# Order of work ahead of the first row gather in a sketch-attention and router kernel

## The chip, the core and the metric

The kernel runs on one core of a Trainium2 chip. The metric is the device time of one launch, in microseconds (us); lower is better. Each engine (TensorE, VectorE, ScalarE, GpSimd, SyncE; PE, DVE, ACT, POOL and SP in the profile) works through its own instruction queue in order. An instruction whose inputs are not ready holds up everything behind it in the same queue.

## What is computed

`q`, `k` and `v` have 4 batches, 4 heads, 1088 tokens and 32 numbers per head. `S1` and `S2` are 8x32 sketches. Attention has no softmax: each key and query becomes 64 features, the products of its 8 numbers under S1 with its 8 under S2. The result has 4352 rows of 128 numbers, and each row goes to one of 8 experts.

```
q_p, k_p = phi(q), phi(k)                    # phi(x)[i*8+j] = (S1 x)[i] * (S2 x)[j]
kv = einsum('bhsf,bhsd->bhfd', k_p, v);  z = sum(k_p, axis=2)
x = (q_p @ kv) / (q_p @ z + 1e-6)            # 4352 rows of 128
logits = (x/|x|) @ (emb/|emb|).T / tau       # 8 experts
e = argmax(logits);  gate = softmax(logits)[e]
out[row] = gate * (relu(x[row] @ w1[e]) @ w2[e])     # w1: 128x1024, w2: 1024x128
```

## The kernel before, in words

**Halves.** Two batches are worked on at a time, so the attention comes in halves m=0 (batches 0, 1) and m=1 (batches 2, 3). In each half the tokens are 17 tiles of 128, taken in groups that begin at tile c0 = 0, 4, 8, 12 (four tiles each) and 16 (one tile). The text writes "group 4" for the group that begins at tile 4.

**A group of queries** goes through these steps in `queries` (L485): `tr` (L494) turns the queries on PE and copies them on ACT; `ab` (L500) multiplies by the sketches; `b` (L505) copies the second factors on ACT (groups 0 and 8 of half 1 copy both factors, L381); `prod` (L512) multiplies the factors, on DVE, or on POOL for groups 0 and 8 of half 1 (L386); `tr_qp` (L538) turns the features on PE (L542) and `qpT` (L545) copies them on ACT (L547); `nd` (L549) multiplies by the sums of the keys on PE (L555); `x` (L562) divides on DVE (L565 to L572). In half 0 the four large groups go another way: `pairs` (L515) makes both factors of all 64 features directly on PE (L522), `seconds` (L527) copies the second factors on ACT (L531), and `prods` (L533) multiplies on DVE (L534).

**Routing.** `router` (L628) picks the expert of each row, counts rows per expert, and `place` (L648) gives each row its place in its expert. A first table (`table(0, ...)`, L726) is made from half 0 alone. It lists the rows of 10 full blocks of 128 rows each with one expert; a second table with 28 blocks comes later, from all rows. The first table's chain is `place` (L654 to L658), `count` (L786, L779), `take` and `split` (L661, L665), `rest` (L789, with `blocks`, L699), `mark` (L674), `find` (L736, the line L744), `digit` twice (L748), `sums` on PE (L754) and `tokens` (L765, three DVE instructions L769 to L771). `tokens` writes two lists of indices: `dst_i`, where an empty lane has the number 8192, and `src_i`, the same cut off at the last row.

**Experts.** `fetch` (L882) gathers the 128 rows of a block from DRAM by an indirect DMA of POOL (L885), `turn` (L889) turns them on PE (L891) and copies them (L893), `up` (L931) is the first layer (L939 on PE, the ReLU L947 on ACT), `down` (L969) the second (L975, L984) and the scatter of the result (L987, which leaves out indices above the last row). The gate comes from `norm` (L949: ACT L952, then a power on POOL, L953), `inverse` (L955, DVE L956 and L957), `shares` (L959, ACT L963) and `share` (L965, DVE).

**What sets the order.** `put_at(tick)(after, rank, f)` (L997) files a piece of work under a tick and a rank. `emit` (L1085) issues the ticks in order and, in a tick, the pieces by rank. Each engine's queue has its instructions in that order. Around the change the pieces are:

- tick 8: turn group 4 of half 1 (53.5), the last keys, `total`, turn group 8 (55.3), `tr_qp` of group 0 (55.5), `tr_kv`, `ab` of group 4 (55.8), `place` (56), `count` (56.5), `take`, `split`, `qpT` of group 0 (58), `rest`, `b` of group 4 (58.7), `mark`, `find`, the two digits, `prod` of group 4 (62.5), turn groups 12 and 16, `nd` of group 0 (84), `ab`, `b` and `prod` of group 8 (84.6 to 84.8), `sums` (85), `tokens` (86), the gathers 0 to 3 (87), `x` of group 0 (90);
- tick 9: `tr_qp` and `qpT` of group 4 (20), `ab` and `b` of groups 12 and 16 (21), `tr_qp` and `qpT` of group 8 (21.5), `nd` of group 4 (30), `turn(0)` (30.21), `nd` of group 8 (30.3), `norm(0)` (30.7), `prod` of groups 12 and 16 (30.8), `x` of group 4 (71) and of group 8 (71.5);
- tick 10: gather 4 (29), `up(0)` (30), `turn(1)` (45), `inverse(0)` (59), `shares(0)` (60), `best` and `pick` for half 1 (72), `norm` of blocks 1 to 3 (74.6);
- tick 11: `tr_qp` and `qpT` of groups 12 and 16 (20), gather 5, `up(1)` (30), `turn(2)` (45), `nd` of groups 12 and 16 (70), `place`, `down(0)` (74).

**PSUM.** The large tiles, `ps_big` (L90), have two buffers, which are taken in turn: each new tile takes the buffer of the tile before the last. `pairs`, `tr_qp` of a large group, `nd`, the table's bank and `up` all take one.

Of the kernel before, what the change touches and what calls it, by code (L numbers as in the profile page):

```python
# [11 lines left out]
F32 = mybir.dt.float32  # L12
BF16 = mybir.dt.bfloat16
I32 = mybir.dt.int32
# [32 lines left out]
NOWHERE = 8192  # L47
# [16 lines left out]
def kernel(  # L64
# [32 lines left out]
    zeros = consts.tile([P, P], F32, name="zeros")  # L97
# [3 lines left out]
    def keep_warm(n):  # L101
        for _ in range(n):
            nc.tensor.matmul(ps_warm[:, :P], zeros, zeros, start=True, stop=True)  # L103
# [15 lines left out]
    nc.scalar.dma_start(tau_sb[:], bass.AP(tensor=tau.tensor, offset=tau.offset, ap=[[0, E], [1, 1]]))  # L119

# [107 lines left out]
    rows = tc.dram_tile([N, ROW], F32, name="rows")  # L228
# [27 lines left out]

    def more_constants():
        nc.vector.memset(ones, 1.0 / P)
        nc.vector.memset(ones_e, 1.0)

        nc.vector.memset(less, -(P - 1) / (2.0 * P))
        nc.vector.memset(more, (P - 1) / (2.0 * P))

        nc.vector.memset(near, -1.0 / (2.0 * P))
        nc.vector.memset(c_early, 0.0)
        nc.vector.memset(w_late, float(KEYS * E))
        for t in (place_k, place_r):
            nc.vector.memset(t, -1.0)

    def iotas():  # L270
# [22 lines left out]
        nc.vector.tensor_copy(digits, tok_i[:, 1:])  # L293
# [191 lines left out]
    def queries(m, c0, c1, put, put_nd):  # L485
# [41 lines left out]
        def seconds(j):  # L527
            if j == 0:
                s["b"] = tile_of(n, [P, 2, w], "qpT")
                s["qpT"] = held[:, c0 // 4].rearrange("p (a n) -> p a n", a=2)  # L530
            nc.scalar.copy(s["b"][:, j].rearrange("p (j n) -> p j n", j=2), s["big"][j][:, :, 2 * P:])  # L531

        def prods(j):  # L533
            nc.vector.tensor_mul(s["qpT"].rearrange("p a (j n) -> p j a n", j=4)[:, 2 * j:2 * j + 2],  # L534
                                 s["big"][j][:, :, :2 * P].rearrange("p j (a n) -> p j a n", a=2),
                                 s["b"][:, j].rearrange("p (j a n) -> p j a n", j=2, a=2))
# [53 lines left out]
        else:  # L590
# [102 lines left out]
    src_i = [consts.tile([P, n], I32, name=f"src_i{i}") for i, n in enumerate(SIZES)]  # L693
# [32 lines left out]
    def table(which, m1, key):  # L726
# [6 lines left out]
        def lie(t):  # L733
            return t if which == 0 else t.rearrange("p n w -> p w n")

        def find():  # L736
            if which == 0:
                s["hit"] = consts.tile([P, n, w], BF16, name="hit0")
                s["col"] = consts.tile([P, 2, n, w], BF16, name="col0")
            else:  # L740

                s["hit"] = work.tile([P, w, n], BF16, tag="xg", bufs=3, name="hit1").rearrange("p w n -> p n w")
                s["col"] = work.tile([P, w, 2, n], BF16, tag="xg", bufs=3, name="col1").rearrange("p w d n -> p d n w")
# [21 lines left out]
        def tokens(k0, k1):  # L765
            ps = s["ps"].rearrange("p (d n) -> p d n", d=2)
            rest = column(f"rest{which}_{k0}", w=k1 - k0)
            to = dst_i[which][:, k0:k1]
            nc.vector.tensor_scalar(rest, ps[:, 1, k0:k1], -1.0, float(NOWHERE), op0=ALU.mult, op1=ALU.add)  # L769
            nc.vector.tensor_sub(to, rest, ps[:, 0, k0:k1])  # L770
            nc.vector.tensor_scalar_min(src_i[which][:, k0:k1], to, N - 1)  # L771
# [110 lines left out]
    def fetch(i):  # L882
# [3 lines left out]
            out=xs[i][:], out_offset=None, in_=rows[:2 * S if t == 0 else N],  # L886
            in_offset=bass.IndirectOffsetOnAxis(ap=src_i[t][:, j:j + 1], axis=0))

    def turn(i):  # L889
# [3 lines left out]
        (nc.scalar.copy if i == 0 or 4 <= i <= 8 else nc.vector.tensor_copy)(xT[i], ps[:, :P])  # L893
# [135 lines left out]
    put(0, 87, lambda: [fetch(i) for i in range(AHEAD)])  # L1029
# [110 lines left out]
```

## Time and profile before

| what | value |
|---|---|
| median of 9 runs | 205.7 us (204.2 to 207.36) |
| the profiled execution's own time | 204.62 us |
| its span, first to last instruction | 202.8 us |
| outside the span | 1.8 us |
| granted TensorE clock | 0.995 |
| busy: PE, DVE, ACT, POOL | 193.8, 91.6, 101.9, 105.5 us |
| bytes moved | 39.42 MB, mean 194 GB/s |

All times in the text that are points on the clock are microseconds from the span's start. The profile gives, for each engine, when instructions began and how long they took (timeline), what an engine waited for (waits), and the chain of waits that ended last, followed back from the last instruction. "x32" after a line is a count of instructions; a matmul on f32 shows as two.

### The profile page before, as it was taken

How to read it: one execution, taken by the hardware profiler on the slowest of the kernel's cores; microseconds unless marked ns; L12 is line 12 of the kernel's file. 1: busy time of each engine (PE TensorE's matmuls, PEld its weight loads, DVE VectorE, ACT ScalarE, POOL GpSimd, SP SyncE). 2: the span in 40 equal slices, each digit the busy share in tenths (PEclk: the TensorE clock that was granted, in tenths of full speed). 3: DMA queues.
4: the chain of work that ended last, by engine and by line, in shares of the span. 5: the costliest groups of instructions: out<-in, count | busy, mean ns of one | idle time of the engine just before them, and what ended most of it. 6: DMA issues, size and time to landing. Idle time of an engine off the chain costs nothing.

```text
span 202.8 us, 6985 instructions
## 1 busy us (share of the span) xinstructions
PE 193.8 (96%) x2592; PEld 183.2 (90%) x2592; DVE 91.6 (45%) x402; ACT 101.9 (50%) x290; POOL 105.5 (52%) x136
## 2 busy tenths in 40 slices
PE   7989999998899999999999999999999999999991
PEld 7658778987799999999999999999999999999991
DVE  5577858978884759942221221222212212112200
ACT  2656442254446546634555554654555546777440
POOL 4010100332745567757786767767767677564043
PEclk9999999999999999999999999999999999999997
DMA  4999899981669478664566466565665796485000
GB/s 124 328 266 313 200 286 278 269 302 39 146 236 290 176 242 263 173 180 106 189 179 205 151 188 192 157 203 172 154 224 150 187 306 238 104 302 196 3 26 25
DMA packets 28160, 39.42 MB, mean 194 GB/s; under 512 B 5737, under 2 KB 21364, under 8 KB 28128
## 3 DMA queue, kind: packets, MB, share of 16 engines
q1 hardware_dynamic: 25776, 34.23, 56.6%
q0 software_dynamic: 2304, 4.74, 7.7%
q8 instruction: 22, 0.36, 0.8%
q14 instruction: 10, 0.08, 0.1%
q10 hardware_dynamic: 48, 0.01, 0.0%
HBM read 34.37 MB, written 4.73 MB: 193 GB/s over the span
## 4 chain that ended last, share of the span: by engine, by line
PE 83%; ACT 4%; DVE 4%; DMA 3%; POOL 3%; issue 1%; POOLq 0%; ACTq 0%; DVEq 0%
PE ps_big L939 27%; PE ps_acc L975 14%; PE ps_ab L975 14%; PE ps_big L944 4%; PE ps_acc L439 4%; PE ps_big L555 3%; DMA xs<-rows,src_i 3%; PE ps_t L353 3%; PE ps_t L891 2%; PE ps_big L522 2%; PE ps_acc L978 2%; PE ps_ab L978 2%; PE ps_ab L370 2%; PE ps_acc L103 1%; ACT qpT L531 1%
## 5 line engine op out<-in xcount | busy, mean ns | idle before, releaser
L939 PE MATMUL ps_big<-xTb,wb 128*128 128x128 f32 x512 | 62.9, 276 | 0.0
L939 PEld LDWEIGHTS ps_big<-xTb,wb 128*128 128x128 f32 x512 | 59.7, 192 | 0.6 <-DVE gate L967 0.2
L987 POOL DMA_INDIRECT out_dram<-y,dst_i x36 | 37.4, 1040 | 41.0 <-ACT y L984 19.9
L947 ACT ACTIVATE hT<-ps_big 128x1024 f32<-128x1024 f32 x36 | 36.9, 1025 | 37.6 <-PE ps_big L939 36.8
L885 POOL DMA_INDIRECT xs<-rows,src_i x36 | 36.7, 1020 | 9.3 <-issue 8.4
L893 DVE COPY xTb<-ps_t 128x128 f32<-128x128 f32 x30 | 8.7, 292 | 59.5 <-PE ps_t L891 59.5
L975 PE MATMUL ps_acc<-w_sb,hT 128*128 x256 | 31.3, 275 | 0.0
L975 PE MATMUL ps_ab<-w_sb,hT 128*128 x256 | 31.2, 275 | 0.0
L975 PEld LDWEIGHTS ps_acc<-w_sb,hT 128*128 128x128 f32 x256 | 29.9, 192 | 0.0
L975 PEld LDWEIGHTS ps_ab<-w_sb,hT 128*128 128x128 f32 x256 | 29.9, 192 | 0.0
L953 POOL TENSOR_TENSOR norm<-norm,half_c 128x1 f32<-128x1 f32 x36 | 21.4, 598 | 2.9 <-ACT sq L952 2.4
L966 DVE TENSOR_SCALAR gate<-gate 128x1 f32<-128x1 f32 x36 | 5.4, 151 | 21.1 <-ACT probs L963 21.1
L984 ACT ACTIVATE y<-ps_acc,gate 128x128 f32<-128x128 f32 x18 | 6.6, 368 | 13.9 <-PE ps_acc L975 12.2
L952 ACT ACTIVATE sq<-xs 128x128 f32<-128x128 f32 x36 | 10.8, 301 | 1.1 <-DMA xs<-rows,src_i 1.0
L984 ACT ACTIVATE y<-ps_ab,gate 128x128 f32<-128x128 f32 x17 | 6.2, 368 | 10.2 <-PE ps_ab L975 8.7
L386 POOL TENSOR_TENSOR kp<-both 128x1024 f32<-128x1024 f32 x1 | 2.0, 1960 | 16.8 <-ACT kb L376 16.8
L963 ACT ACTIVATE probs<-xs,norm 128x8 f32<-128x8 f32 x36 | 10.6, 295 | 0.0
L891 PE MATMUL ps_t<-ident,xs 128*128 128x128 f32 x36 | 10.2, 282 | 0.0
L439 PEld LDWEIGHTS ps_acc<-v,kp 128*64 128x64 f32 x256 | 8.3, 137 | 1.7 <-issue 1.4
L386 DVE TENSOR_TENSOR kp<-ps_ab,kb 128x1024 f32<-128x1024 f32 x7 | 8.5, 1220 | 2.7 <-ACT kb L376 2.3
L439 PE MATMUL ps_acc<-v,kp 128*64 128x64 f32 x256 | 9.5, 225 | 0.3
L386 POOL TENSOR_TENSOR qp<-both 128x1024 f32<-128x1024 f32 x2 | 4.0, 1982 | 7.8 <-ACT both L381 7.8
(237 smaller groups left out, 298.5 us busy)
## 6 DMA issues: line engine op xcount, KB each, us to landing
wb<-in_moe_w_dram SPq DMA_DIRECT2D x36, 512.0 KB, 3.8
w_sb<-in_moe_w_dram SPq DMA_DIRECT2D x16, 256.0 KB, 5.4
rows<-xg SPq DMA_DIRECT2D x4, 544.0 KB, 4.3
v<-in_v_dram SPq DMA_DIRECT2D x4, 512.0 KB, 6.5
v<-in_moe_w_dram SPq DMA_DIRECT2D x4, 512.0 KB, 4.7
k<-in_k_dram SPq DMA_DIRECT2D x3, 512.0 KB
q<-in_q_dram SPq DMA_DIRECT2D x3, 512.0 KB
xs<-rows,src_i POOLq DMA_INDIRECT x36, 3.8
```

What stands on the lines that cost most here:

```text
L386: engine.tensor_mul(t.rearrange("p j h (i k) -> p (j h) i k", i=R), ab[:, :, 0].unsqueeze(3).broadcast_to([P, n * H, R, R]), b.unsqueeze(2 ...
L439: nc.tensor.matmul(acc[m][u * HALF:(u + 1) * HALF, i, p], s["kp"][:, c - c0, h], bass.AP(tensor=vo.tensor, offset=vo.offset, ap=[list(vo.a ...
L885: nc.gpsimd.indirect_dma_start(out=xs[i][:], out_offset=None, in_=rows[:2 * S if t == 0 else N], in_offset=bass.IndirectOffsetOnAxis(ap=sr ...
L891: nc.tensor.transpose(ps[:, :P], xs[i][:, :DM], ident)
L939: nc.tensor.matmul(ps[:, u, j * P:(j + 1) * P], w[:, f * P:(f + 1) * P], x, start=True, stop=True)
L947: nc.scalar.activation(hT[i], ps, ACT.Relu)
L952: nc.scalar.activation(sq, xs[i][:, :DM], ACT.Square, accum_out=norms[i])
L953: nc.gpsimd.tensor_tensor(out=norms[i], in0=norms[i], in1=half_c, op=ALU.pow)
L963: nc.scalar.activation(p, xs[i][:, DM:], ACT.Exp, scale=norms.pop(i)[:, 0:1], accum_out=gate[i])
L975: nc.tensor.matmul(ps, h[:, f * P:(f + 1) * P], ws[0][:, f], start=f == 0, stop=f == NF - 1)
L984: nc.scalar.activation(y, ps, ACT.Copy, scale=gate.pop(i)[:, 0:1])
L987: d = nc.gpsimd.indirect_dma_start(out=out[:, :], out_offset=bass.IndirectOffsetOnAxis(ap=dst_i[t][:, j:j + 1], axis=0), in_=y[:], in_offs ...
```

## The change

Seven edits:

1. `ab` and `b` of group 4 of half 1 move from behind `tr_qp` of group 0 to ahead of it (ranks 55.25 and 55.27), and so ahead of `place` and `count`.
2. The first table's `hit` and `col` get the layout of the second table: blocks innermost, where tiles were innermost.
3. The row numbers are stored negative, an empty lane's number is 4352, and one more matmul in `sums` (`ones` by `nowhere`) starts the sum at 4352. `tokens` is then one sum over the two digits instead of three instructions, and one list of indices, `dst_i`, serves both gather and scatter. This holds for both tables.
4. `rows` gets a 4353rd row of zeros, which empty lanes gather; a DMA on ACT's queue writes it at the start. `zeros` grows from 128 to 136 columns for it.
5. The first gather goes alone; `prod` of group 8 on POOL moves behind it (rank 87.05), and the gathers 1 to 3 behind that (87.1).
6. In ticks 9 and 10 `nd` of group 4 moves ahead of `turn(0)`, `tr_qp` and `qpT` of group 8 behind `turn(0)`, and `nd` and `x` of group 8 from ahead of `up(0)` to behind it. Block 1's turned rows are copied by ACT, not DVE.
7. In `pairs`, the two halves of every second bank change places, so that the second factors of a pair of banks lie side by side, 512 columns in a row. `seconds` and `prods` read accordingly.

```diff
-NOWHERE = 8192
+NOWHERE = N
...
-    zeros = consts.tile([P, P], F32, name="zeros")
+    zeros = consts.tile([P, ROW], F32, name="zeros")
...
+    rows = tc.dram_tile([N + 1, ROW], F32, name="rows")
+    nc.scalar.dma_start(rows[N:N + 1], zeros[:1])
...
+    nowhere = [consts.tile([P, 2, n], BF16, name=f"nowhere{n}") for n in (EARLY, LATE + SHARED)]
...
+        for t, n in zip(nowhere, (EARLY, LATE)):
+            nc.vector.memset(t, 0.0)
+            nc.vector.memset(t[:, 0, :n], float(NOWHERE))
...
-        nc.vector.tensor_copy(digits, tok_i[:, 1:])
+        nc.vector.tensor_scalar_mul(digits, tok_i[:, 1:], -1.0)
...
-                        nc.tensor.matmul(s["big"][j // 2][u * HALF:(u + 1) * HALF, j % 2, t * 2 * P:(t + 1) * 2 * P],
+                        at = (t ^ j % 2) * 2 * P
+                        nc.tensor.matmul(s["big"][j // 2][u * HALF:(u + 1) * HALF, j % 2, at:at + 2 * P],
...
-            nc.scalar.copy(s["b"][:, j].rearrange("p (j n) -> p j n", j=2), s["big"][j][:, :, 2 * P:])
+            nc.scalar.copy(s["b"][:, j], s["big"][j].rearrange("p j n -> p (j n)")[:, 2 * P:6 * P])
...
-                                 s["big"][j][:, :, :2 * P].rearrange("p j (a n) -> p j a n", a=2),
+                                 bview(s["big"][j], [[6 * P, 2], [P, 2], [1, P]]),
...
-                       {tr: (8, 53.5), ab: (8, 55.8), b: (8, 58.7), prod: (8, 62.5), tr_qp: (9, 20), qpT: (9, 20),
-                        nd: (9, 30), x: (9, 71)},
-                       {tr: (8, 55.3), ab: (8, 84.6), b: (8, 84.7), prod: (8, 84.8), tr_qp: (9, 21.5), qpT: (9, 21.6),
-                        nd: (9, 30.3), x: (9, 71.5)},
+                       {tr: (8, 53.5), ab: (8, 55.25), b: (8, 55.27), prod: (8, 62.5), tr_qp: (9, 20), qpT: (9, 20),
+                        nd: (9, 21.4), x: (9, 71)},
+                       {tr: (8, 55.3), ab: (8, 84.6), b: (8, 84.7), prod: (8, 87.05), tr_qp: (9, 30.25), qpT: (9, 30.27),
+                        nd: (10, 31), x: (10, 31.5)},
...
         def lie(t):
-            return t if which == 0 else t.rearrange("p n w -> p w n")
+            return t.rearrange("p n w -> p w n")
...
+            nc.tensor.matmul(s["ps"], ones, nowhere[which].rearrange("p d n -> p (d n)"), start=True, stop=False)
             for t in tiles:
-                nc.tensor.matmul(s["ps"], row[:, :, t], s["col"].rearrange("p d n w -> p (d n) w")[:, :, t], start=t == tiles[0], stop=t == tiles[-1])
+                nc.tensor.matmul(s["ps"], row[:, :, t], s["col"].rearrange("p d n w -> p w d n")[:, t].rearrange("p d n -> p (d n)"),
+                                 start=False, stop=t == tiles[-1])
...
-            nc.vector.tensor_scalar(rest, ps[:, 1, k0:k1], -1.0, float(NOWHERE), op0=ALU.mult, op1=ALU.add)
-            nc.vector.tensor_sub(to, rest, ps[:, 0, k0:k1])
-            nc.vector.tensor_scalar_min(src_i[which][:, k0:k1], to, N - 1)
+                nc.vector.reduce_sum(out=dst_i[which][:, k0:k1], in_=ps[:, :, k0:k1].rearrange("p d n -> p n d"), axis=AX.X)
...
-            out=xs[i][:], out_offset=None, in_=rows[:2 * S if t == 0 else N],
-            in_offset=bass.IndirectOffsetOnAxis(ap=src_i[t][:, j:j + 1], axis=0))
+            out=xs[i][:], out_offset=None, in_=rows[:2 * S if t == 0 else N + 1],
+            in_offset=bass.IndirectOffsetOnAxis(ap=dst_i[t][:, j:j + 1], axis=0))
...
-        (nc.scalar.copy if i == 0 or 4 <= i <= 8 else nc.vector.tensor_copy)(xT[i], ps[:, :P])
+        (nc.scalar.copy if i < 2 or 4 <= i <= 8 else nc.vector.tensor_copy)(xT[i], ps[:, :P])
...
-    put(0, 87, lambda: [fetch(i) for i in range(AHEAD)])
+    put(0, 87, lambda: fetch(0))
+    put(0, 87.1, lambda: [fetch(i) for i in range(1, AHEAD)])
```

More of the change, by code (lines that the diff above doesn't have):

```diff
@@ L102, in keep_warm @@
         for _ in range(n):
-            nc.tensor.matmul(ps_warm[:, :P], zeros, zeros, start=True, stop=True)
+            nc.tensor.matmul(ps_warm[:, :P], zeros[:, :P], zeros[:, :P], start=True, stop=True)
     for _ in range(7):
@@ L226 @@
     nc.gpsimd.memset(half_c, 0.5)
-    rows = tc.dram_tile([N, ROW], F32, name="rows")
     def iota(shape, pattern, base, mult, name):
@@ L692 @@
     SIZES = (EARLY, LATE)
-    src_i = [consts.tile([P, n], I32, name=f"src_i{i}") for i, n in enumerate(SIZES)]
     dst_i = [consts.tile([P, n], I32, name=f"dst_i{i}") for i, n in enumerate(SIZES)]
@@ L733, in lie @@
         def lie(t):
-            return t if which == 0 else t.rearrange("p n w -> p w n")
+            return t.rearrange("p n w -> p w n")
         def find():
[L737 to L743, printed above, removed]
+            pool = consts.tile if which == 0 else lambda *a, **k: work.tile(*a, tag="xg", bufs=3, **k)
+            s["hit"] = pool([P, w, n], BF16, name=f"hit{which}").rearrange("p w n -> p n w")
+            s["col"] = pool([P, w, 2, n], BF16, name=f"col{which}").rearrange("p w d n -> p d n w")
             nc.vector.tensor_tensor(out=lie(s["hit"]), in0=lie(key().unsqueeze(2).broadcast_to([P, n, w])),
@@ L766, in tokens @@
             ps = s["ps"].rearrange("p (d n) -> p d n", d=2)
-            rest = column(f"rest{which}_{k0}", w=k1 - k0)
-            to = dst_i[which][:, k0:k1]
-            nc.vector.tensor_scalar(rest, ps[:, 1, k0:k1], -1.0, float(NOWHERE), op0=ALU.mult, op1=ALU.add)
-            nc.vector.tensor_sub(to, rest, ps[:, 0, k0:k1])
-            nc.vector.tensor_scalar_min(src_i[which][:, k0:k1], to, N - 1)
+            with nc.allow_low_precision(reason="whole numbers of at most NOWHERE"):
+                nc.vector.reduce_sum(out=dst_i[which][:, k0:k1], in_=ps[:, :, k0:k1].rearrange("p d n -> p n d"), axis=AX.X)
         return find, lambda: digit(0), lambda: digit(1), sums, tokens, first_rows, halves
```

## The prediction

> **What bounds it now.** I read the busy table first, then the chain of waits from 40 to 66 us, then the timelines of DVE, ACT and PE there.
>
> ```profile
> PE 193.8 (96%) x2592; PEld 183.2 (90%) x2592; DVE 91.6 (45%) x402; ACT 101.9 (50%) x290; POOL 105.5 (52%) x136
> PE   7989999998899999999999999999999999999991
> ```
>
> PE is busy for 193.8 of 202.8 us. Of the 9.0 us without a matmul, 0.8 lie ahead of the first instruction and 4.2 behind the last matmul (198.6 to 202.8), so some 4 are holes. From 64.6 us on PE has none until its last layer. So what counts is when PE enters that stretch, which is when `nd` of group 12 starts (L555 at 62.66): the same matmuls come before it and after it in both kernels. Only the matmul that the change adds to each table alters PE's own work.
>
> ```profile
> 44.83 0.62 PE ps_ab L370 x16
> 45.45 0.14 PE ps_big L654
> ...
> 49.10 0.41 DVE col L748 x2
> ...
> 49.83 1.13 DVE qp L386
> ...
> 51.07 0.18 DVE dst_i L770
> ...
> 51.27 0.17 DVE src_i L771
> ...
> 51.75 1.20 POOL xs L885
> ```
>
> The chain runs from the counts through unbroken DVE work to the first gather. Then the ends at the stretch that matters, on DVE, ACT and PE:
>
> ```profile
> 59.57 0.14 DVE L956 TENSOR_SCALAR norm<-norm 128x1 f32<-128x1 f32 x1
> 59.75 0.16 DVE L957 RECIPROCAL norm<-norm 128x1 f32<-128x1 f32 x1
> ```
>
> ```profile
> 59.25 1.02 ACT L947 ACTIVATE hT<-ps_big 128x1024 f32<-128x1024 f32 x1 [2.73 <-PE ps_big L939]
> 60.17 0.29 ACT L963 ACTIVATE probs<-xs,norm 128x8 f32<-128x8 f32 x1
> 61.62 0.99 ACT L547 COPY qpT<-ps_big 128x1024 f32<-128x1024 f32 x1
> ```
>
> ```profile
> 57.19 2.02 PE L939 MATMUL ps_big<-xTb,wb 128*128 128x128 f32 x16
> 60.33 2.05 PE L939 MATMUL ps_big<-xTb,wb 128*128 128x128 f32 x16
> ```
>
> `up(0)` starts at 57.19, its ReLU at 59.25, and ACT then works without a gap: exponential, three squares, the copy L547 of group 12. `inverse(0)` on DVE is over at 59.91, just before ACT wants it. PE's L555 follows the copy at 62.66. From `up(0)` to that L555 it is 5.47 us, and the last wait there is for ACT.
>
> **The parts.**
>
> *Counts.* `ab` of group 4 (0.62) leaves the place between L454 and L654. Ahead of L542, PE waited for POOL's product until 43.6; last keys end at 42.84, so `ab` and the turn of group 8 (0.5) now end near 43.96 and L542 starts 0.33 later. Gain 0.62 - 0.33 = 0.3. The copy `b` (0.27) moves ahead of ACT's copies for group 8 and group 0; the latter (L547 at 45.03, then the key copies at 46.25) stays within 0.1, since what it copies is also later by 0.3 and `b` no longer follows it.
>
> *Table.* `hit` is f32 in both layouts and keeps 0.34. The two digits took 0.245 each for 180 elements. In the new layout the second table shows 1.36 for 1152, as long as its f32 `hit`: 1.04 ns an element and some 0.16 on top, so 180 elements need 0.34. Loss 2 x 0.10 = 0.2. `sums` on PE (17 matmuls from 49.58) still ends before DVE's product of group 4, which is next on the chain, so the unit steps and the extra matmul (0.06) are hidden; the second table's extra matmul costs PE 0.06.
>
> *Tokens.* From the product's end (50.89) to `src_i` (51.44) three instructions took 0.55. One sum over 20 numbers is between the 0.17 of such small instructions and the 0.24 of L710 over 80: 0.2. Gain 0.35. Indices come 0.3 - 0.2 + 0.35 = 0.45 earlier, at 51.0; tr_qp of group 4 gains only 0.3 - 0.2 = 0.1.
>
> *POOL.* The first gather goes at 51.3 instead of 51.75; it did not wait for POOL's product, which ended at 51.34, less than the 0.3 that POOL takes from indices to gather. In the new place it would have, so the move is right for gather 0. Behind it the product (1.96) holds gathers 1 to 3 and `norm(0)`: 51.3 + 1.2 + 2.0 + 0.3 = 54.8 for gather 1 (before 53.25), then 56.05 and 57.3.
>
> *Up.* Gather 0 was there at the latest 3.84 after its start (L891 at 55.59); the median of all gathers is 3.8, their range 3.2 to 4.7. So `turn(0)` runs at 55.1 (54.5 to 56.0), and on PE the turn of group 8 (0.92 and a switch of 0.1) and `up(0)` are queued behind it: 56.2. A second condition: `up(0)` now takes the `ps_big` buffer of `nd` of group 4, free when DVE's `x` has read it. That is behind `prod` of groups 12 and 16, which ran from 53.45 to 55.01 and come 0.15 earlier; with 1.38 from L565 to the end of L571 it is 56.2 too. So `up(0)` starts at 56.27, 0.9 earlier than 57.19.
>
> *What is late next.* `nd` and `x` of group 8 now lie behind `up(0)`, and `x` is ahead of `inverse(0)` in DVE's queue. Behind `inverse(0)` wait ACT's exponential, squares and L547, then PE's L555. From the start of `up(0)`: its 16 matmuls 1.86; a switch 0.05; L555 to the first instruction of `x` 1.41 (54.30 to 55.71); `x` 1.71 (55.71 to 57.42); `inverse` 0.34; to ACT 0.05; from the exponential to L555 of group 12 2.49 (60.17 to 62.66). Sum 7.9 in place of 5.47. So L555 of group 12 starts at 56.27 + 7.9 = 64.15, against 62.66: 1.5 later. PE has only `up(1)` to put there (60.93 for its buffer, so 61.0 to 62.9) and then stands for over 1 us. Gathers 1 to 3 hide in that: even at 4.7 they land by 59.5, 60.75 and 62.0, against PE's `turn(1)` near 59.3 and ACT's squares after 61.6. With ACT copying block 1 (0.27 near 59.6) nothing is late: ACT stands there anyway. Should that cover go, the copy costs 0.27.
>
> *Pairs.* ACT's copy of 512 columns in two pieces takes 590 ns (L531), one in a single piece also 590 (L355): nothing. A copy waited for nearly all of its 32 matmul halves (the chain has x32, x26 and x27 before L531). If it now waits only for the second factors it starts 0.55 earlier. But next in ACT's queue is the copy of turned keys, whose turn on PE follows all the pairs: 8.86, 12.44 and 16.09 against 8.89, 12.54 and 16.12 now. So at most 0.03 + 0.1 + 0.03, some 0.15; if the keys' copies were not held so, 3 x 0.55 = 1.65. I take 0.05, near the first. The Trainium skill (PSUM — Partial Sum Buffer, "PSUM bank collisions raise a hardware error") tells against any of it: an engine may not read a bank quadrant while TensorE writes it, whatever the columns, and here both banks are still being written. By it the gain is 0; by the chain's rows 0.15 at most.
>
> *At the start.* The pad row is one more issue on ACT's queue, by the three there 0.28 to 0.58, ahead of the table load at 2.10 (1.28 long); ACT's first copy is at 5.36, so it is hidden, and would cost as much with that cover gone. Eight more columns of `zeros` cost 0.01. Four memsets (0.07 each) fill DVE's 0.82 wait for the sketches. The negated digits keep their 0.2. An empty lane's row instead of the last one: no row here shows a difference; gathers of 128 rows have 0.95 to 1.45 on POOL whatever the rows, so 0, at worst 0.5 on POOL, which is idle 48% of the span.
>
> Sum: 1.5 + 0.06 - 0.05 - 0.1 (that `tr_qp` of group 4, and with it DVE's part, might be a little earlier yet than counted) = 1.4 later. The profiled execution's 204.6 (202.8 and 1.8 around it) would be 206.0. The median of the runs shown is 1.1 above that execution: 205.7 + 1.4 = **207.1**. About 0.5%, 1.03 us, is what a measurement here can tell from no change.
>
> **The rivals.**
>
> *A. Smaller loss, 206.4.* `up(0)` is held neither by `x` of group 4 nor by the gather. POOL's product ends at 54.5, so the turn of group 8 ends at 55.5 and `up(0)` starts then: 55.5 + 7.9 = 63.4, a loss of 0.75. For it: gathers land in 3.2 at best. Against it: two buffers taken in turn, and `up(0)` at 57.19 before right after L571 ended (57.09).
>
> *B. Not slower, 205.2.* `inverse(0)` doesn't decide when ACT goes on, and PE's own work does. From 56.27: 1.86 + 1.19 + 0.11 + 1.17 + 1.89 + 0.11 = 6.3, L555 at 62.6, nothing lost; from 55.5 it is 61.8, a gain of 0.85, and with the pairs' 0.15 and an earlier gather 1.0 or more: 204.7. It decides if the exponential can start by 60.1. For it: the holes of PE at 48.8 (0.8) and 52.7 (0.5) do shrink. Against it: DVE's order.
>
> *C. The change doesn't do what it says: no earlier rows, 208.0.* Gather 0 takes 4.7, as one beside the weights' loads did: `turn(0)` at 56.0, `up(0)` at 57.15, a loss of 2.3.
>
> **Chances.** Forecast 0.47 (206.6 to 207.9; 0.45 slower, 0.02 within), A 0.22 (0.18 within, 0.04 slower), B 0.20 (0.14 faster, 0.06 within), C 0.11 (slower). So slower 0.60, within 0.5% 0.26, faster 0.14. The range 204.9 to 208.3 leaves out the better half of B and a C with a still later gather. Slower alone: 206.6 to 208.3.
>
> **What would show it.** Right: L654 near 45.1; two L748 of 0.34; indices near 51.0, the first gather near 51.3, the second near 54.8; `up(0)` near 56.3; L956 of block 0 near 61.3, behind L572; ACT idle for over 1 us before the first L963; L555 of group 12 near 64.1. Wrong: an exponential at 60.2 or earlier, or a PE without the hole after `up(1)`. L531 starting 0.5 earlier than the pairs' end would show the pairs' part larger than I took it.

## The result, and the profile after

The changed kernel takes 207.19 us (median of 20 runs, 206.36 to 211.09); the kernel before takes 205.25 us (median of 62 runs, 203.98 to 207.36). The ratio is 1.0099, with a 95% interval of [1.0079, 1.012]: slower by 2.0 us (205.25 x 0.0099), 1.6 to 2.5. Ratios and intervals here compare only runs in the faster of two states that executions fall into, so they differ a little from the quotient of the medians. The profiled execution of after took 207.25 us with a span of 205.5 us and a granted clock of 0.999.

In the page of after, the busy table and PE's row of slices answer to those of before:

```profile
PE 194.0 (94%) x2594; PEld 183.6 (89%) x2594; DVE 92.3 (45%) x399; ACT 102.4 (50%) x291; POOL 105.6 (51%) x136
PE   7989999997787999999999999999999999999991
```

PE is busy for 0.2 us more, and the span is 2.7 us longer. So 2.5 us are new holes. PE's row shows where: a slice is 5.1 us, and the slices from 46 to 67 us now have 7, 7, 8 and 7 tenths, where before had 8, 8, 9 and 9.

The chain of waits up to the first gather (start, duration, what):

```profile
45.17 0.10 PE ps_big L664 x3
...
48.69 0.60 DVE col L751 x2
...
49.61 1.13 DVE qp L393
50.74 0.08 DVE dst_i L773
...
51.12 3.32 DMA xs<-rows,dst_i
54.48 0.33 PE ps_t L893
```

The counts are earlier, the two digits are longer (0.60 for both, 0.41 in before), one sum stands where three instructions stood, and gather 0 is there 3.32 us after its start. Up to here all is as forecast. Then DVE's timeline, POOL's beside it, and the ends on PE and ACT (start, duration, engine, line, operation; the idle time ahead of it and what ended it in brackets):

```profile
52.73 1.61 DVE L727 TENSOR_SCALAR exp_i<-exp_f 1x10 int32<-1x10 f32 x1
54.26 1.53 DVE L393 TENSOR_TENSOR qp<-ps_ab,qb 128x1024 f32<-128x1024 f32 x2
...
60.55 0.17 DVE L573 TENSOR_SCALAR rc<-ps_big 128x16 f32<-128x16 f32 x1 [3.05 <-PE ps_big L563]
...
62.27 0.14 DVE L958 TENSOR_SCALAR norm<-norm 128x1 f32<-128x1 f32 x1
```

```profile
51.12 1.20 POOL L887 DMA_INDIRECT xs<-rows,dst_i  x1 [7.66 <-DVE c_early L800]
52.36 1.95 POOL L393 TENSOR_TENSOR qp<-both 128x1024 f32<-128x1024 f32 x1
```

```profile
57.19 2.02 PE L941 MATMUL ps_big<-xTb,wb 128*128 128x128 f32 x16 [1.50 <-ACT sq L954]
...
65.15 1.36 PE L563 MATMUL ps_big<-kz,qpT 128*64 128x82 f32 x32 [0.97 <-ACT qpT L555]
```

```profile
62.64 0.30 ACT L965 ACTIVATE probs<-xs,norm 128x8 f32<-128x8 f32 x1 [1.57 <-DVE norm L959]
```

Two things are to be seen. First, L727 (L720 before), which turns ten experts' numbers of one row into integers, took 0.15 us in before and takes 1.61 us here. It ends within 0.03 us of POOL's product (52.36 + 1.95 = 54.31), and DVE's products of groups 12 and 16 stand behind it. Second, the inverse of block 0's norm (L958) runs only after the `x` of group 8 (60.55 to 62.35), and ACT stands 1.57 us for it. The profile puts `up(0)`'s wait down to ACT's square (over at 57.10), but DVE's `x` of group 4 has read the buffer at the same moment (57.09); E2 and E6 tell the two apart. The copy behind ACT's exponential releases L563 of group 12 (`nd`) at 65.15, where before had it at 62.66. That is 2.49 later; some 0.2 of it is there from the start (the first pairs begin at 7.38 instead of 7.14, which varies from 6.4 to 7.4 over the executions profiled, in both kernels' versions; at 42 us PE is still 0.2 behind). From that `nd` to the span's end it is 140.1 us in before and 140.35 in after.

### The profile page after: what moved, and what is told of

It is laid out like the page before. It is cut to its first block, busy times and chain, and to the rows that moved or that the text cites. A ratio compares the mean times of both kernels' runs of the same rounds, so it can differ in the third digit from the quotient of the medians.

```text
span 205.5 us, 6989 instructions
## 1 busy us (share of the span) xinstructions
PE 194.0 (94%) x2594; PEld 183.6 (89%) x2594; DVE 92.3 (45%) x399; ACT 102.4 (50%) x291; POOL 105.6 (51%) x136
## 4 chain that ended last, share of the span: by engine, by line
PE 84%; DVE 7%; ACT 4%; DMA 2%; issue 2%; POOL 1%; POOLq 0%; ACTq 0%; DVEq 0%
PE ps_big L941 27%; PE ps_acc L977 14%; PE ps_ab L977 14%; PE ps_big L946 4%; PE ps_acc L446 4%; PE ps_big L563 3%; PE ps_t L360 3%; PE ps_t L893 2%; PE ps_big L530 2%; PE ps_acc L980 2%; PE ps_ab L980 2%; PE ps_ab L377 2%; DMA xs<-rows,dst_i 2%; PE ps_acc L103 1%; DVE kp L393 1%
## 5 line engine op out<-in xcount | busy, mean ns | idle before, releaser
L887 POOL DMA_INDIRECT xs<-rows,dst_i x36 | 36.8, 1021 | 15.5 <-DVE c_early L800 7.7
L946 PE MATMUL ps_big<-xTb,wb 128*64 128x64 f32 x128 | 7.9, 224 | 0.0
```

What stands on the lines that cost most here:

```text
L887: nc.gpsimd.indirect_dma_start(out=xs[i][:], out_offset=None, in_=rows[:2 * S if t == 0 else N + 1], in_offset=bass.IndirectOffsetOnAxis(a ...
L946: nc.tensor.matmul(ps[r, u, j * P + b * HALF:j * P + (b + 1) * HALF], wh[:, f * P + c * HALF:f * P + (c + 1) * HALF], x[:, b * HALF:(b + 1 ...
```

## The experiments

The theory after the first look: the loss lies in the order of ticks 8 to 10 (parts 5 and 6), by two mechanisms. **The hold:** the product of group 8 now runs on POOL when DVE reaches L727, which stands until it ends. **The late inverse:** DVE divides group 8 ahead of `inverse(0)`. Rivals: the table, the pad row or the pairs cost the time; or the gather decides, and the rest is cover.

E1 to E4 ran on a chip where before took 207.79 us (29 runs), E5 to E8 on one with 205.47 (29 runs), E9 and E10 on one with 205.13 (11 runs), E11 and E12 on one with 205.35 (23 runs). So times of different chips are compared by their ratios only, and the points on the clock in the table, which are of different chips and starts too, to about a microsecond. The column "code packet" is the start of the one packet that the instruction queue q8 moves in this stretch, from the DMA view; it lasts 0.9 to 1.4 us. Its part comes out with E9.

| kernel | DVE's experts (L720, L727) | gather 0 start, PE's turn of it | code packet | `up(0)` | first exponential | `nd` of group 12 | ratio |
|---|---|---|---|---|---|---|---|
| before | 0.15 | 51.75, 55.59 | 54.9 | 57.19 | 60.17 | 62.66 | 1 |
| after | 1.61 | 51.12, 54.48 | 53.9 | 57.19 | 62.64 | 65.15 | 1.0099 [1.0079, 1.012] |
| E1 | 0.15 | 51.18, 56.51 | 57.4 | 57.55 | 63.43 | 65.93 | 1.0105 [1.0069, 1.0141] |
| E2 | 1.62 | 51.17, 54.69 | 53.9 | 57.24 | 61.01 | 64.15 | 1.0006 [0.9981, 1.0031] |
| E3 | 0.15 | 50.62, 55.55 | 56.8 | 56.58 | 60.63 | 63.98 | 1.004 [1.0012, 1.0069] |
| E4 | 0.15 | 51.43, 56.87 | 54.8 | 58.97 | 61.95 | 64.44 | 0.9989 [0.9965, 1.0014] |
| E5 | 0.15 | 51.34, 56.59 | 54.4 | 58.14 | 61.15 | 63.64 | 0.9974 [0.9936, 1.0011] |
| E6 | 0.15 | 50.20, 53.79 | 53.0 | 55.32 | 59.09 | 62.36 | 0.9992 [0.9956, 1.0027] |
| E7 | 0.21 | 50.87, 56.68 | 54.6 | 58.03 | 64.73 | 67.23 | one run |
| E8 | 0.15 | 51.60, 55.45 | 54.6 | 57.05 | 60.03 | 62.52 | 0.9994 [0.9958, 1.003] |
| E9 | 1.62 | 51.28, 56.65 | 54.5 | 58.62 | 64.41 | 66.91 | 1.0148 [1.01, 1.0196] |
| E10 | 0.15 | 50.47, 54.25 | 53.0 | 55.85 | 61.24 | 63.75 | 1.0131 [1.0091, 1.0172] |
| E11 | 0.38 | 52.14, 57.15 | 54.3 | 58.75 | 61.74 | 64.22 | 1.0043 [1.0002, 1.0084] |
| E12 | 0.15 | 51.30, 55.08 | 54.8 | 56.68 | 59.66 | 62.15 | 0.9944 [0.9908, 0.9981] |

### E1: the experts' numbers ahead of the product

```diff
-    put(1, 21, lambda: early["experts"]())
+    put(0, 87.6, lambda: early["experts"]())
```

> The changed kernel with one piece moved: the small DVE instruction that writes the first table's experts (L727, 1.61 us there in place of 0.15) goes ahead of x of group 0 (rank 87.6 of tick 8), where POOL still issues the first gather and its product has not begun. Theory: DVE was held in it by POOL's product (52.36 to 54.31), and up(0) waits for DVE's x of group 4 behind it. Then L727 takes 0.15, the products of groups 12 and 16 begin near 53.2, up(0) near 56.2 in place of 57.19, and nd of group 12 near 64.15 in place of 65.15: 1.0 us less than the changed kernel, ratio to before 1.005. Rival: up(0) is held by something that is not DVE (its weights, ACT's square that also ended at 57.09); then L727 is short, up(0) stays at 57.2 and the ratio at 1.010.

The time did not move: 209.91 us, ratio 1.0105. DVE's timeline and PE's:

```profile
51.08 0.15 DVE L727 TENSOR_SCALAR exp_i<-exp_f 1x10 int32<-1x10 f32 x1
```

```profile
56.51 0.33 PE L893 MATMUL ps_t<-ident,xs 128*128 128x128 f32 x1 [2.10 <-DMA xs<-rows,dst_i]
```

The hold is real: ahead of the product L727 takes 0.15, and DVE's products of groups 12 and 16 start at 53.28, 1.0 earlier. But L727 also gives SP the numbers with which it loads the weights of blocks 1 and 2. SP issued its three loads from 50.45 to 53.03 here, and from 50.39 to 56.14 in after. The gather then took 5.3 us. The DMA view by queue says why. Its columns are packets, MB and share of the 16 engines; q1 has the weights and q0 the gathers. First after, from 52 to 53 us and from 53 to 54 us, then the gathers' queue in E1 from 55 to 56 us, while q1 had 93% of the engines:

```profile
q1 hardware_dynamic: 89, 0.35, 88.5%
```

```profile
q0 software_dynamic: 27, 0.07, 33.0%
q1 hardware_dynamic: 25, 0.05, 13.6%
```

```profile
q0 software_dynamic: 19, 0.03, 8.1%
```

The gather is 32 packets: 16 with eight rows each (4352 bytes) and 16 of 4 bytes, one behind each of them. In after 27 of them go within one microsecond, when block 0's weights are through, since the next loads are held with L727; the 32nd is through at 54.1. In E1 the next loads fill the engines, and the 32nd is through at 56.2. PE's turn follows some 0.35 us after it in both. So the hold costs DVE 1.5 us and shields the gather; undoing it alone gains nothing. What `up(0)` waits for E1 can't tell, since the gather was later still.

### E2: the inverse ahead of the late division

```diff
-                    put(0, 59, lambda: inverse(0))
+                    put(0, 31.4, lambda: inverse(0))
```

> The changed kernel with inverse(0) ahead of x of group 8 on DVE (rank 31.4 in place of 59, tick 10). Theory: ACT's exponential, squares and copy of group 12 wait for that inverse. It then is over before 59, the exponential runs behind block 1's copy near 61.05 in place of 62.64, ACT is ready for nd of group 12 near 63.5, and PE's own up(1) and turn(2), over near 64.05, decide: nd of group 12 near 64.1 in place of 65.15, 1.05 us less, ratio 1.005. Rival: the place of the matmuls on PE alone costs the time (nd of group 8 behind up(0)), and ACT would be late anyway: nd of group 12 stays near 65.1, ratio 1.010.

It took 207.68 us, ratio 1.0006. DVE's and ACT's timelines:

```profile
58.66 0.15 DVE L958 TENSOR_SCALAR norm<-norm 128x1 f32<-128x1 f32 x1 [1.10 <-issue]
```

```profile
61.01 0.30 ACT L965 ACTIVATE probs<-xs,norm 128x8 f32<-128x8 f32 x1
```

All up to `up(0)` is as in after, L727's hold too. `up(0)` starts at 57.24, 0.1 behind DVE's `x` (57.14) and before ACT's square ends (57.29), so it is DVE that it waits for. The inverse comes 3.6 earlier, ACT no longer stands for it, and `nd` of group 12 comes at 64.15, 1.0 earlier than in after and where it was expected. The ratio is better than the 1.005 expected: by it the loss is gone, though `nd` is still 1.5 later than in the trace of before. That trace is of another chip, and on E2's chip, where before takes 2.5 us more, before was not profiled; so where the rest was regained is open. One rank of one pair of small DVE instructions is worth 1.0 us by the traces and 1.9 by the ratios of after and E2.

### E3: both

E3 has the edits of E1 and E2.

> The changed kernel with both moves. Theory: up(0) near 56.2, x of group 8 over near 61.0, up(1) near 61.05, nd of group 12 near 63.1: 2.0 us less than the changed kernel and 0.45 more than before, ratio 1.002. Rival of one cause: no more than the better of the two single moves, ratio 1.005.

It took 208.79 us, ratio 1.004. Against E1 on the same chip the early inverse gains 1.1 us (209.91 to 208.79), as much as it did in E2. Against E2 the early experts lose 1.1 (207.68 to 208.79; the two intervals overlap), although in the profiled execution `nd` of group 12 was no later (63.98). That execution was 1.4 us under the kernel's own median (207.4), so the trace does not show the loss; what it does show is the gather's 4.9 us beside the loads.

### E4: the old order with all other parts

```diff
-                        nd: (9, 21.4), x: (9, 71)},
+                        nd: (9, 30), x: (9, 71)},
...
-                       prod: (8, 87.05), tr_qp: (9, 30.25), qpT: (9, 30.27), nd: (10, 31), x: (10, 31.5)},
+                       prod: (8, 84.8), tr_qp: (9, 21.5), qpT: (9, 21.6), nd: (9, 30.3), x: (9, 71.5)},
...
-        (nc.scalar.copy if i < 2 or 4 <= i <= 8 else nc.vector.tensor_copy)(xT[i], ps[:, :P])
+        (nc.scalar.copy if i == 0 or 4 <= i <= 8 else nc.vector.tensor_copy)(xT[i], ps[:, :P])
```

> The changed kernel with the order of the groups 4 and 8 in ticks 8 to 10 as before (POOL's product ahead of the first gather, nd and x of group 8 ahead of up(0), block 1 copied by DVE); counts, table, indices, pad row and pairs stay changed. Theory: all of the loss lies in that order. POOL's product runs from 49.3 to 51.3 and may hold DVE's small c_early for 0.4; the first gather starts near 51.6, x of group 0 0.2 to 0.6 earlier than before, up(0) near 56.4 to 57.0 and nd of group 12 near 61.9 to 62.5: ratio 0.996 to 0.999. Rival: table, row sum or pairs cost part of the loss: ratio 1.003 or more.

It took 207.69 us, ratio 0.9989. So the counts, table, indices, pad row and pairs together cost nothing that can be measured, and gain nothing either. Half of what the earlier indices gain is lost on POOL, as the timelines of DVE and POOL show:

```profile
50.74 0.54 DVE L800 TENSOR_SCALAR c_early<-upto 128x8 f32<-128x8 f32 x1
```

```profile
49.30 1.95 POOL L393 TENSOR_TENSOR qp<-both 128x1024 f32<-128x1024 f32 x1 [5.84 <-ACT both L388]
```

The indices are there at 50.8 (51.4 in before), but the product holds POOL until 51.25; the gather starts 0.3 earlier than in before and is used 5.4 later (why so late comes out with E9). Another small tensor_scalar, L800, stands until the same product's end (0.54 instead of 0.15 in after).

### E5, E6 and E8: later loads

In all three the experts' numbers move to rank 70 of tick 9, so that the loads of blocks 1 and 2 come later: E5 is E4 with that edit, E6 is E2 with it, E8 is the kernel before with it.

```diff
-    put(1, 21, lambda: early["experts"]())
+    put(1, 70, lambda: early["experts"]())
```

> The fourth experiment (old order of groups 4 and 8, new table and indices) with the first table's experts written later, behind DVE's products of groups 12 and 16 (rank 70 of tick 9 in place of 21), so that SP issues the loads of blocks 1 and 2 near 55.5 in place of 53.9. Second theory: the rows of gather 0 move only when no weights are loading (they came 3.3 us after the gather's start with nothing beside them, 5.3 to 5.4 with the loads of blocks 1 and 2), so gather 0 lands near 54.9 in place of 56.8, up(0) starts near 56.6 in place of 58.97, and the ratio to before is 0.992 to 0.996. Rival: gather 0 takes over 5 us there for another cause, such as the gathers 1 and 2 right behind it; up(0) stays near 58.9 and the ratio near 0.999.

> The changed kernel with inverse(0) ahead of x of group 8, as in the second experiment, and the experts behind the products of groups 12 and 16 (rank 70), where POOL's product is over and the loads of blocks 1 and 2 are not issued before 55. Second theory: both causes that the first three experiments showed are out of the way: no DVE instruction is held (0.15 for the experts, products from 53.2), gather 0 lands near 54.6, up(0) near 56.3, up(1) near 61.0 and nd of group 12 near 63.1 in place of 64.15: 1.0 us less than the second experiment, ratio 0.996 to 0.998 on this chip. Rival: the loads, now later, come too late for up(1), or the gathers 1 to 3 land too late beside them; ratio 1.000 or more.

> The kernel before with only the experts of the first table moved behind the products of groups 12 and 16 (rank 70 of tick 9). Second theory: gather 0 had landed by 55.59 there and up(0) waits for x of group 4, so nothing is won but a little on gathers 1 to 3: the loads start near 55.8 in place of 54.05, land near 60.1, just in time for up(1) at 60.3; ratio 0.998 to 1.001. Rival: the later loads alone make a kernel faster, ratio below 0.997, and a gain of the fifth experiment would be theirs.

They took 204.71, 205.09 and 205.27 us; the ratios are 0.9974, 0.9992 and 0.9994, and each interval holds 1. The profiled execution of E5 took 207.27 us, 2.6 over its median, so only the early part of its trace is used.

E8 shows that later loads alone gain nothing. E6 removes both mechanisms and the loss is gone: L727 comes after the product and takes 0.15, `up(0)` is at 55.32, 0.1 behind DVE's `x` and 0.7 before ACT's square begins (55.99), and the exponential 3.8 later, no longer 5.5 later as in after. E2, which keeps the hold, has the same ratio within the intervals (1.0006), so these runs show no time that the hold itself costs. There is no gain over before either, since ACT's last square waits 0.76 for gather 3, which starts behind the product, and the two `up`s and turns in front of `nd` of group 12 fill PE until 62.29. E5 fell short of what was expected of it: though the loads were late, PE's turn still came 5.2 after gather 0's start.

### E7: the same numbers by a sum

```diff
-            nc.vector.tensor_scalar_min(exp_i[which], f, float(E - 1))
+            with nc.allow_low_precision(reason="whole numbers"):
+                nc.vector.reduce_sum(out=exp_i[which][:], in_=le[0:1], axis=AX.X)
```

> The changed kernel with the experts of the first table made by a sum over the comparison (DVE tensor_reduce, 80 numbers) at the same place in the queue, in place of the tensor_scalar; the cut at the last expert is left out. Theory of the held instruction: only a DVE operation that can use its second pair of memory ports waits for POOL's product, and a reduce can't; it takes 0.25 in place of 1.61, right at 52.7, while POOL's product runs. Rival: DVE as a whole stands there, whatever the operation; it ends with POOL's product near 54.3 again. By the second theory the loads of blocks 1 and 2 then come near 53.6 and gather 0 lands later than 54.4.

One run took 209.59 us. DVE's timeline, in which POOL's product runs from 52.11 to 54.06:

```profile
52.48 0.21 DVE L728 TENSOR_REDUCE exp_i<-le 1x10 int32<-1x80 f32 x1
52.98 1.55 DVE L393 TENSOR_TENSOR qp<-ps_ab,qb 128x1024 f32<-128x1024 f32 x2 [0.28 <-ACT qb L383]
```

In the midst of POOL's product a sum on DVE takes 0.21, and a product with one operand in PSUM starts too, as soon as ACT's copy is there. So it is the kind of instruction that is held, not DVE. The Trainium skill (SBUF — State Buffer, "Who interferes with whom") gives this rule: DVE's second pair of SBUF ports is GpSimd's only one, tensor_scalar from SBUF can use both pairs when its operands meet certain conditions, and whichever started first keeps the shared pair for its whole instruction, while on trn2 tensor_reduce never contends. The runs agree with it: 1.61, 1.62 and 1.62 us for L727 or L720 inside the product (after, E2, E9), 0.21 for the sum. Not every tensor_scalar is held: in before two ran inside POOL's product of 49.32 to 51.34 without delay, L717 on a single number (0.14) and L769, which reads PSUM (0.15). As in E1 the loads came early, and PE's turn came 5.8 after the gather's start.

### E9: the order alone

Parts 5 and 6 on the kernel before, and nothing else.

```diff
-                        nd: (9, 30), x: (9, 71)},
+                        nd: (9, 21.4), x: (9, 71)},
...
-                       prod: (8, 84.8), tr_qp: (9, 21.5), qpT: (9, 21.6), nd: (9, 30.3), x: (9, 71.5)},
+                       prod: (8, 87.05), tr_qp: (9, 30.25), qpT: (9, 30.27), nd: (10, 31), x: (10, 31.5)},
...
-    put(0, 87, lambda: [fetch(i) for i in range(AHEAD)])
+    put(0, 87, lambda: fetch(0))
+    put(0, 87.1, lambda: [fetch(i) for i in range(1, AHEAD)])
```

> The kernel before with parts 5 and 6 of the change alone (the product behind the first gather, the order of ticks 9 and 10, block 1's copy on ACT); the counts, the table, the indices, the pad row and the pairs stay as before. Theory: the loss lies in the order. Indices as before near 51.4, gather 0 near 51.75, POOL's product from 53.0 to 54.9; the one-row tensor_scalar of the blocks' experts (L720) begins at 53.35, inside the product, and stands until it ends; the products of groups 12 and 16 then run from 54.9 to 56.4, the part of x of group 4 that frees the buffer ends near 57.8, up(0) starts at 57.85 and L555 of group 12 another 7.95 later, at 65.8, which is 3.1 after that of before. Ratio 1.010 to 1.016, no less than that of the whole change. Rival 1, the loss lies in the other five parts (digits, pad row, one more matmul, pairs): ratio 1.000 within 0.002. Rival 2, the order costs only what the late division costs and L720 isn't held: L720 0.15, up(0) at 57.2 or earlier, ratio near 1.006.

It took 208.68 us, ratio 1.0148. DVE's and PE's timelines:

```profile
52.87 1.62 DVE L720 TENSOR_SCALAR exp_i<-exp_f 1x10 int32<-1x10 f32 x1
```

```profile
56.65 0.48 PE L891 MATMUL ps_t<-ident,xs 128*128 128x128 f32 x1 [2.54 <-DMA xs<-rows,src_i]
```

The order alone makes the loss, and both mechanisms are there (a hold of 1.62, an exponential 5.8 after `up(0)`). Rivals 1 and 2 fall. One thing does not fit: the loads were held with L720, and still PE's turn came 5.4 after the gather's start, so that `up(0)` was 0.8 later than forecast. The DMA view of E9 from 54 to 55 us and from 55 to 56 us shows what lies there:

```profile
q8 instruction: 1, 0.02, 5.7%
q0 software_dynamic: 3, 0.00, 0.2%
```

```profile
q0 software_dynamic: 1, 0.00, 0.1%
```

31 of the 32 packets have begun by 54.2, and the last rows are through at 54.52. From there one packet of q8 occupies one DMA engine for 0.9 us (5.7% of 16 us), to 55.43, and the gather's last packet, of 4 bytes, goes 0.01 behind it. The chain of waits shows that PE's turn waited for the gather's landing and for nothing after it:

```profile
51.28 5.33 DMA xs<-rows,src_i
56.60 0.04 issue
56.65 0.48 PE ps_t L891
```

The gather reports landing with 16 semaphore updates. In E9's trace 15 are in by 54.50, and the last comes at 56.60, 1.2 after the end of the q8 packet. E4, E5 and E7 are alike: 4 bytes of a gather go 0.01 behind the q8 packet, gather 0's last report comes 1.2 to 1.3 after that packet's end (56.82, 56.55, 56.63), and PE's turn 0.04 later. In after, E1, E2, E3 and E6 it comes 0.3 after the gather's 32nd packet. Why it takes 1.2 and not 0.3 behind a q8 packet the traces don't show. The span has 22 packets of q8, 16 KB each, and PE does 2592 matmuls and as many weight loads in it, some 240 instructions a packet; no other engine has more than 402 instructions by the profile's count. So q8 is taken to bring PE's code. Theory c, then: E4, E5, E7 and E9 waited not for the rows but for the last report, which stood behind a code packet.

There is a second cost. The windows view gives a granted clock of 1.00 in E9 up to 56 us, 0.50 from 57 to 59 and 0.89 to 61; while PE stood for 2.5 us it went to half speed, and `up(0)` took 2.35 (2.02 in after). In E7 it was 0.50 to 0.55 from 58 to 61, and `up(0)` took 3.27.

### E10: gather 0 alone

E5 with the gathers 1 to 3 behind the norm of block 0.

```diff
-    put(0, 87.1, lambda: [fetch(i) for i in range(1, AHEAD)])
+    put(1, 30.75, lambda: [fetch(i) for i in range(1, AHEAD)])
```

> The changed kernel with the order of before (parts 5 and 6 undone) and the loads of the weights of blocks 1 and 2 late, and now the gathers 1 to 3 behind the norm of block 0, so that gather 0 is alone beside the load of block 0. In the same kernel with the gathers right behind, gather 0 took 5.2 from its start to PE's L893, though blocks 1 and 2 were loaded late. Theory a: the gathers behind it share its time. Then gather 0 from 51.3 is there after 3.3 to 3.6, L893 follows nd of group 4 near 55.2, up(0) starts near 56.8 in place of 58.1, but gather 1 begins only near 56.8 and PE's turn(1) waits for it until 60.5. Ratio 0.996 to 1.001. Theory b: the load of block 0 alone holds it: still about 5, L893 near 56.5, up(0) near 58.1, and the later gathers make it slower, 1.003 to 1.007.

It took 207.67 us, ratio 1.0131. PE's timeline:

```profile
54.25 0.33 PE L893 MATMUL ps_t<-ident,xs 128*128 128x128 f32 x1
...
60.29 0.33 PE L893 MATMUL ps_t<-ident,xs 128*128 128x128 f32 x1 [2.41 <-DMA xs<-rows,dst_i]
```

The gather is there within 3.8 us, and PE doesn't wait for it, as theory a has it. But the code packet began at 53.0 here, and the gather's 32nd packet was through at 53.3 all the same, so the packet was not in its way, and the run doesn't tell theory a from theory c. The time was forecast wrongly (0.996 to 1.001): PE's 2.41 of waiting for gather 1 cost far more than the early `up(0)` gave. Whether all of the loss of 2.7 us is that wait the trace doesn't settle, as it also has a hole of 1.2 late in the span that E8's has too (1.1), at no loss there.

### E11 and E12: the code packet moved

E5 with another number of warming matmuls on PE at the start, which fill the same time: E11 has 20 matmuls more, E12 six fewer (0 and 7 in place of the 31 and 2 shown for E11).

```diff
-    for _ in range(7):
+    for _ in range(31):
...
-    keep_warm(6)
+    keep_warm(2)
```

> The changed kernel with the order of before and the late loads (as in the run whose gather 0 took 5.2), and at the start 31 small and 2 large warming matmuls in place of 7 and 6: as long as before (about 3.5 us, while PE waits for the first keys) but 20 matmuls more, so that PE's later instructions lie 80 places further on. Theory c: PE's code comes in packets of 16 KB on a queue of its own, one for each 240 to 285 of its instructions; in that run one of 0.85 us lay at 54.4, between the gather's data and its last packet, and PE's turn of block 0 followed 1.3 us after it. Moved by 80 instructions, the packet lies near 52, turn(0) follows the gather's last packet by 0.3 and comes right behind nd of group 4, near 55.2; up(0) near 56.8, nd of group 12 near 62.5. Ratio 0.990 to 0.995. Theory a, the gathers 1 to 3 close behind share its time: L893 still near 56.5, up(0) near 58.1, ratio 0.996 to 0.999.

> The same kernel with 0 small and 7 large warming matmuls, 6 matmuls fewer, so that PE's code packet comes 24 instructions later: near 55.0 instead of 54.4. Theory c: the gather's last packet is through by 54.6 and is no longer behind it, so turn(0) comes behind nd of group 4 near 55.2, up(0) near 56.8, nd of group 12 near 62.5, ratio 0.990 to 0.996; unless PE itself lacks its next instructions by then, which would show as idle time put down to issue. Theory a: L893 near 56.5, up(0) near 58.1, ratio 0.996 to 0.999.

E12 took 203.97 us, ratio 0.9944 [0.9908, 0.9981], faster than before. PE's timeline:

```profile
55.08 0.33 PE L893 MATMUL ps_t<-ident,xs 128*128 128x128 f32 x1
...
56.68 2.02 PE L941 MATMUL ps_big<-xTb,wb 128*128 128x128 f32 x16
```

As theory c had it, the packet is at 54.8, the turn comes behind `nd` of group 4 without a wait, and `up(0)` is at 56.68; all 32 packets of the gather are through by 54.1, ahead of the code packet. The gathers 1 to 3 are as close behind as in E5, so theory a falls. That it was the six matmuls that moved the packet is not shown: E4, with as many matmuls as E5, has it at 54.8 too. And by the runs' times E5 and E12 are not told apart, as their intervals overlap.

E11 took 206.58 us, ratio 1.0043. Its packet came at 54.3 and not near 52, so twenty matmuls more did not move it as theory c had it. Gather 0's last report came at 56.42, again 1.2 after the packet's end, but PE was in `nd` of group 4 until 57.15: its clock was 0.50 from 53 to 56 us in the profiled execution, with no long hole ahead of it. What lowered it was not found, so the time tells nothing of theory c. Nor is it explained that L727 took 0.38 there.

## Why the prediction was right, point by point

The sign, the place and the size held: 207.1 was forecast, with a loss of 1.4, and 207.19 was measured, with a loss of 2.0 [1.6, 2.5]. The medians meet more closely than the losses because the nine runs of before lay 0.45 above its larger sample.

- *Counts, digits, tokens: right.* L662 (the old L654) at 44.98 for 45.1; two digits 0.60 for 0.68; the sum 0.15 for 0.2; indices at 50.8 for 51.0. Gather 0 at 51.12 for 51.3, gather 1 at 54.48 for 54.8. As this execution ran 0.2 late up to 42 us, the counts in truth gained 0.6 where 0.3 was forecast (E4 and E12 show 0.6 too): in part because the moved matmuls hold L542 (L550 in after) up by 0.2 and not by the 0.33 of the sum.
- *The gather: right in after.* 54.48 for 55.1, at the edge of its range (54.5 to 56.0). Rival C (4.7 and more) did not come in after, but nearly the same kernels had it: E1 and E3 by the loads, E9 by a code packet. What rival C put down to loads alone has two causes.
- *`up(0)`: the step that failed.* The prediction had DVE's products of groups 12 and 16 "0.15 earlier", at 53.3, and hence `up(0)` at 56.27. The products began at 54.26, because of L727, and `up(0)` came at 57.19. Of the 0.92, some 0.2 is the later start of this execution and 0.7 the hold. The prediction listed what waits behind POOL's product on POOL and on PE, and gave no thought to what DVE does beside it. The trace of before had the sign in its DVE and POOL timelines, at a product of keys:

```profile
37.59 1.96 POOL L386 TENSOR_TENSOR kp<-both 128x1024 f32<-128x1024 f32 x1 [16.75 <-ACT kb L376]
```

```profile
38.93 0.65 DVE L670 TENSOR_SCALAR place_k<-mx 128x8 f32<-128x8 f32 x1
...
46.59 0.17 DVE L670 TENSOR_SCALAR place_k<-mx 128x9 f32<-128x9 f32 x1
```

The same small tensor_scalar takes 0.17 by itself (with a ninth column) and 0.65 inside the product, and ends 0.03 behind it (39.55).
- *From `up(0)` to `nd` of group 12: right.* 7.96 for 7.9, by the late inverse. ACT stood 1.57 before the first exponential, for "over 1 us". E2 shows that this is the cause: the inverse moved, 6.9 remain and by the ratio the loss is gone within [-0.2%, +0.3%]. Rival B, PE's own work, is refuted as the limit in after; in E2 it is the limit (PE's turn of block 2 runs right up to `nd`, ACT's copy is over at 63.46).
- *The hold and the gather, together.* The missed hold cost 0.7 at `up(0)` in the trace, and shielded the gather. So the gather came at 54.48, and with the hold away it would have come at 56.5 (E1). Two unforeseen effects nearly cancelled, and part of the good agreement is luck.
- *Pairs: right, nothing gained.* The chain of after, at the second set of pairs:

```profile
10.74 1.37 PE ps_big L530 x26
...
12.14 0.60 ACT qpT L539
```

The copy still waits for nearly all of the matmuls, 1.37 us of them as in before, and takes as long. That is what the PSUM rule named in the prediction would have it be; the trace doesn't tell whether the chip or a wait in the program sets it.
- *At the start: right.* The pad row's DMA takes ACT's queue from 2.10 to 2.36, and ACT's first copy is at 5.37, as before (5.36).

E12, which has the old order, the late loads and the code packet out of the way, is the one kernel shown to be faster than before, by 0.2 to 0.9%; it is one interval of twelve and was not repeated. In its trace `nd` of group 12 is 0.5 earlier than in before, and `nd` of group 4 is so already (53.78 for 54.30). E4 and E5 have that lead at `nd` of group 4 too (53.91, 53.83) and lose it at `turn(0)`, behind the code packet. So by the traces the five other parts do bring PE some 0.5 us ahead by then; that they make E12 faster is argued from this, not tried.

## What to carry to other kernels

When an elementwise product is moved on GpSimd, look at what VectorE does in its new place: a small tensor_scalar from SBUF to SBUF there can stand until the product ends, as L727 did for 1.6 us, and all that is queued behind it stands too. When a filler is moved behind a critical step, follow it on each engine that it uses: the matmuls of group 8 did no harm, and their division, ahead of a reciprocal that ACT wanted, cost 1 us. And when a gather seems late, look at its packets in the trace, and at its last report, before a cause is named: other loads, a code packet or the gather itself look alike in the chain of waits.

## What was not expected of the hardware

A tensor_scalar of 10 elements on one partition took 1.61 us instead of 0.15, until GpSimd's product over SBUF ended (after, E2, E9), and one of 128x8 took 0.54 (E4) and one 0.65 (before, L670); a tensor_reduce took 0.21 in the same place (E7), and tensor_scalars on a single number or from PSUM were not held (0.14 and 0.15, before).

A packet of what is taken to be TensorE's code held one DMA engine for 0.9 to 1.4 us. Where it fell between a gather's rows and the 4 bytes behind them, the gather's last report came 1.2 to 1.3 us after the packet's end instead of 0.3 after the gather's last packet (E4, E5, E7, E9).

After holes of 2.5 to 2.6 us without a matmul the granted clock was 0.50 for some 3.4 us (E9, E7); with the hole of 2.4 us in E10 and those of 1.5 us and less in after it stayed at 1.00. In E11 it was 0.50 as long with no such hole ahead of it, so the hole is not shown to be the cause.
